# Loading an output projection over all 128 partitions in natural order, with one permuting product added

## The chip, the cores and the metric

The kernel runs on one core of one Trainium2 chip. The metric is the device time of one execution in microseconds (us). Every run is compared with runs of the kernel before on the same chip.

## The reference

A decode step of a gated mix of two branches. Only branch A matters here:

```python
x: (2, 1, 1024)   k_cache, v_cache: (2, 32, 16384, 128)   wq: (1024, 4096)   wo: (4096, 1024)   # bf16
q = (x @ wq) as (2, 32, 1, 128)
p = softmax(q . k_cache * 128 ** -0.5)
o = p . v_cache                                   # (2, 32, 1, 128)
a = o as (2, 1, 4096) @ wo
b = ...                                           # a small mixer and MLP branch
g = sigmoid((x * gate_w).sum(-1))
return g * a + (1 - g) * b
```

The two caches are 537 MB, so the kernel is a stream of cache tiles. `wo` (8.39 MB) comes last: nothing follows it but its own product and a 4 KB store.

One caution on correctness. Branch A averages 16,384 values and is, by the scales of the inputs, far smaller than branch B, so bf16 rounding of the output can hide it. That the changed kernel's permutation is right was therefore also worked through by index on random numbers in double precision (largest difference 1e-12).

## The kernel before

32 tiles of K and 32 of V, each [128 partitions, 32768] bf16, go through three buffers that `wo` shares. Everything is issued on one queue. Cuts are marked.

```python
WO_SPLIT = [16, 8, 4, 2, 1, 1]

def load_wo():
    t = big_tile("wo")[:].rearrange("p (r n) -> p r n", n=D)
    src = A_wo.rearrange("(h a r) n -> h a r n", a=4, r=32)      # head h, quarter a, row r in it
    r0 = 0
    for n in WO_SPLIT:
        for a in range(4):                                        # partition 32a + h
            nc.sync.dma_start(
                out=t[32 * a : 32 * a + 32, r0 : r0 + n, :], in_=src[:, a, r0 : r0 + n, :]
            )
        r0 += n
# ... (cut: other loads, K and V stages) ...
def wo_stage():
    Q = const.tile([P, B, 32], BF16)
    for b in range(B):
        nc.vector.transpose(out=Q[:, b, :], in_=OT[:, b, :])      # 32x32 blocks: Q[32a+h, b, r]
    wo = wt.pop("wo").rearrange("k r (p c) -> k r p c", c=KC)
    for r in range(32):
        for c in range(KC):                                       # 256 products
            nc.tensor.matmul(wo_acc[:, c, :], lhsT=wo[:, r, :, c], rhs=Q[:, :, r],
                             start=(r == 0 and c == 0), stop=(r == 31 and c == KC - 1))
# ... (cut) then fin = wo_acc * g, out_pm = fin + pre, one store
```

The transpose of 32x32 blocks leaves head h, quarter a on partition 32a + h. To meet it, `wo` is loaded in that order: four DMAs for each of six pieces, each to 32 neighbouring partitions.

## Time and profile before

Three runs gave a median of 1365.45 us (1365.17 to 1367.84).

| | kernel before |
|---|---|
| span of the profiled run | 1364.4 us |
| wo issued (the last K tile has been used, a buffer is free) | 1296.9 us |
| last V tile landed, its products begin | 1326.7 us |
| first half of wo landed | 1345.15 us |
| 256 wo products | 1345.4 to 1361.5 us |
| finish and store | 2.9 us |

The page's picture of the span, in 40 slices of 34 us. DMA is the busy share of 16 DMA engines in tenths, GB/s is what they moved:

```profile
DMA  9999999999999999999999999999999999999995
GB/s 400 439 442 431 429 431 423 437 431 439 429 437 431 431 435 437 431 429 429 429 433 444 431 431 433 429 431 435 437 429 429 433 431 437 441 431 430 431 255 139
```

The engines are busy until the last slice, so the memory queue bounds the kernel, but the last two slices move far less than 430 GB/s. The table of stretches shows that tail closer. Its columns are the stretch, its length, busy us of each engine (PE, PEld, which is PE's weight load, DVE, ACT, POOL) with the number of instructions, the granted TensorE clock, the DMA busy share, GB/s:

```profile
1280.00:1297.00 17.00, 15.14 (x54) 5.51 (x54) 15.85 (x14) 0.00 (x0) 0.00 (x0) 0.92 1.00 432
...
1310.00:1315.00 5.00, 0.00 (x0) 0.00 (x0) 0.00 (x0) 0.00 (x0) 0.00 (x0) 0.50 0.96 210
1315.00:1320.00 5.00, 0.00 (x0) 0.00 (x0) 0.00 (x0) 0.00 (x0) 0.00 (x0) 0.50 0.86 172
...
1330.00:1335.00 5.00, 3.34 (x44) 2.02 (x36) 0.37 (x2) 0.59 (x1) 0.00 (x0) 0.94 0.95 202
```

Read the last two columns together: a share of 0.96 with 210 GB/s says that packets are in flight but each takes twice as long. The packet records say it too: a 65,536-byte packet of a V tile takes 2.42 us in the stream and about 4.9 us (median) after 1305 us, once wo has begun. From 1335 to 1355 us the share is lower too, 0.61 to 0.68 at 133 to 204 GB/s: there some engines also stood idle.

The chain of waits that ended last (start us, us, what):

```profile
1296.92 0.34 SPq L127
...
1298.23 46.92 DMA wo<-in_A_wo_dram
1345.15 0.25 issue
1345.40 7.64 PE wo_acc L382 x125
1353.04 0.38 issue
1353.42 8.08 PE wo_acc L382 x131
1361.74 0.23 DVE out_pm L523
```

47 us of transfer and 16 us of products. In the timeline, the last V tile's products:

```profile
1326.73 5.56 PE L342 MATMUL O<-Vn,PT 128*32 128x512 bf16 x64 [19.22 <-DMA Vn<-in_A_v_cache_dram]
```

PE idled 19 us for that tile; the one before it had landed at 1295.2, and tiles come 19.4 us apart in the stream. So this tile too is late, by 12 us.

### The profile page before, as it was taken

What the parts mean: (1) busy time and instruction counts of PE and PEld (TensorE: products, weight loads), DVE (VectorE), ACT (ScalarE), POOL (GpSimd) and SP (SyncE); (2) the same over time, 40 slices, a digit from 0 to 9 for tenths busy, and PEclk for the clock granted to TensorE, in tenths of its full rate; (3) what the DMA queues carried; (4) which work ended last, traced back from release to release, by engine and by line L of the source; (5) the groups of instructions that cost most, each with busy time, mean ns of one, the idle gap of its engine ahead of it and who ended that gap; (6) DMA issues with size and microseconds to landing.
All of it is one profiled execution on the core that took longest, in us unless ns stands there. A gap on an engine that the chain in (4) does not pass through costs nothing.

```text
span 1364.4 us, 12947 instructions
## 1 busy us (share of the span) xinstructions
PE 829.0 (61%) x5523; PEld 401.0 (29%) x5586; DVE 707.2 (52%) x862; ACT 45.6 (3%) x100; POOL 14.5 (1%) x45
## 2 busy tenths in 40 slices
PE   2577665557665666555556755566656555666535
PEld 2233222423224232222223522232222222322215
DVE  0666656256661565654545445566555455666510
ACT  0000000000000000000000000000000000000000
POOL 0000000000000000000000000000000000000000
PEclk9988887688885888777778677888777788887766
DMA  9999999999999999999999999999999999999995
GB/s 400 439 442 431 429 431 423 437 431 439 429 437 431 431 435 437 431 429 429 429 433 444 431 431 433 429 431 435 437 429 429 433 431 437 441 431 430 431 255 139
DMA packets 11833, 573.36 MB, mean 420 GB/s; under 512 B 2176, under 2 KB 2176, under 8 KB 2560
## 3 DMA queue, kind: packets, MB, share of 16 engines
q1 hardware_dynamic: 11776, 572.54, 98.8%
q8 instruction: 43, 0.70, 0.2%
q14 instruction: 14, 0.11, 0.0%
HBM read 572.53 MB, written 0.00 MB: 420 GB/s over the span
## 4 chain that ended last, share of the span: by engine, by line
PE 28%; DVE 23%; DMA 20%; another core or an unknown queue 13%; issue 13%; ACT 2%; SPq 0%; ACTq 0%; POOL 0%
DVE T L290 19%; DMA Kn<-in_A_k_cache_dram 16%; PE S L298 14%; PE O L342 7%; DMA wo<-in_A_wo_dram 3%; PE misc L434 3%; PE misc L352 2%; PE misc L205 2%; ACT Pr L326 1%; DVE PT L330 1%; PE wo_acc L382 1%; ACT Os L350 1%; DVE mx L319 1%; DVE mdiag L312 1%
## 5 line engine op out<-in xcount | busy, mean ns | idle before, releaser
L298 PE MATMUL S<-T,z 128*128 128x512 bf16 x1985 | 583.6, 422 | 340.2 <-DVE T L290 320.4
L290 DVE STREAM_TRANSPOSE T<-Kn 128x1024 f32<-128x1024 f32 x512 | 611.8, 1229 | 267.5 <-DMA Kn<-in_A_k_cache_dram 217.2
L298 PEld LDWEIGHTS <-z 128*128 128x128 bf16 x2048 | 219.2, 107 | 699.2 <-issue 538.0
L342 PE MATMUL O<-Vn,PT 128*32 128x512 bf16 x2048 | 119.7, 387 | 19.2 <-DMA Vn<-in_A_v_cache_dram 19.2
L369 DVE TENSOR_TENSOR OT<-misc,rinv 128x2 bf16<-128x2 f32 x32 | 5.1, 159 | 171.0 <-PE misc L352 171.0
L342 PEld LDWEIGHTS <-PT 128*32 128x32 bf16 x2048 | 73.1, 140 | 65.2 <-DMA Vn<-in_A_v_cache_dram 19.3
L205 PE MATMUL misc<-rs,ones_f 128*128 128x2 f32 x64 | 17.9, 349 | 76.5 <-DVE rs L362 76.5
L350 ACT COPY Os<-O 128x512 f32<-128x512 f32 x32 | 18.8, 586 | 1100.9 <-PE O L342 1100.9
L352 PE MATMUL misc<-osel,Os 128*128 128x2 f32 x256 | 33.7, 254 | 22.2 <-ACT Os L350 22.2
L352 PEld LDWEIGHTS misc<-osel,Os 128*128 128x128 f32 x256 | 31.0, 191 | 36.7 <-ACT Os L350 36.7
L309 DVE TENSOR_REDUCE m<-S 128x1 f32<-128x512 f32 x32 | 22.2, 693 | 36.9 <-PE S L298 36.9
L434 PEld LDWEIGHTS <-wt 128*128 128x128 bf16 x576 | 35.7, 171 | 18.7 <-DMA wt<-in_B_w_dram 17.4
L205 PEld LDWEIGHTS misc<-rs,ones_f 128*128 128x128 f32 x64 | 16.1, 312 | 81.2 <-issue 78.4
L330 DVE STREAM_TRANSPOSE PT<-Pr 128x512 bf16<-128x512 bf16 x32 | 22.7, 711 | 28.7 <-ACT Pr L326 28.7
L326 ACT ACTIVATE Pr<-S,nb 128x512 bf16<-128x512 f32 x32 | 22.0, 687 | 124.4 <-DVE nb L321 121.4
L205 PE MATMUL misc<-mdiag,ones_f 128*128 128x128 f32 x64 | 15.6, 325 | 15.6 <-DVE mdiag L312 15.6
L319 DVE TENSOR_REDUCE mx<-misc 64x1 f32<-64x64 f32 x64 | 14.2, 222 | 19.0 <-PE misc L205 18.6
L268 POOL TENSOR_TENSOR z<-qsel,own 128x32 bf16<-128x32 bf16 x32 | 10.8, 338 | 1225.6 <-PE S L298 1194.3
L382 PE MATMUL wo_acc<-Q,wo 128*128 128x2 bf16 x256 | 15.7, 198 | 11.7 <-DMA wo<-in_A_wo_dram 11.4
L243 PE MATMUL misc<-xT,wt 128*128 128x2 bf16 x256 | 7.1, 165 | 25.8 <-DVE xT L238 23.1
L434 PE MATMUL misc<-xn2T,wt 128*128 128x2 bf16 x224 | 14.4, 202 | 9.1 <-DMA wt<-in_B_w_dram 9.1
L382 PEld LDWEIGHTS <-wo 128*128 128x128 bf16 x256 | 15.6, 169 | 11.8 <-issue 11.8
(70 smaller groups left out, 92.8 us busy)
## 6 DMA issues: line engine op xcount, KB each, us to landing
wt<-in_B_w_dram SPq DMA_DIRECT2D x2, 7168.0 KB, 50.4
wt<-in_B_w_dram SPq DMA_DIRECT2D x2, 2048.0 KB, 40.1
wo<-in_A_wo_dram SPq DMA_DIRECT2D x4, 1024.0 KB, 40.9
wo<-in_A_wo_dram SPq DMA_DIRECT2D x4, 512.0 KB, 49.1
wo<-in_A_wo_dram SPq DMA_DIRECT2D x4, 256.0 KB, 15.8
Kn<-in_A_k_cache_dram SPq DMA_DIRECT2D x32, 52.1
Vn<-in_A_v_cache_dram SPq DMA_DIRECT2D x32, 37.6
wo<-in_A_wo_dram SPq DMA_DIRECT2D x4, 128.0 KB, 6.0
```

Of the source, the lines that this page charges most:

```text
L205: nc.tensor.matmul(ps[:], lhsT=ones_f[:], rhs=src, start=True, stop=True)
L290: nc.vector.transpose(out=T[:].rearrange("p w j s -> p j w s"), in_=Kw[:, m * CW : (m + 1) * CW].rearrange("p (j w e) -> p j w e", w=2, e=32),
L298: nc.tensor.matmul(S[:], lhsT=z[:, v, NM - 1 - m : NM - 1 - m + P], rhs=Tb[:, v // 2, :, v % 2], start=(m == 0 and v == 0), stop=(m == NM ...
L309: nc.vector.reduce_max(out=m[:], in_=S[:], axis=AX.X)
L319: nc.vector.reduce_max(out=mx[pa, :], in_=mall[pa, pa], axis=AX.X)
L326: nc.scalar.activation(out=Pr[:], in_=S[:], func=ACTF.Exp, bias=nb[:], scale=scale, accum_out=rs[:])
L330: nc.vector.transpose(out=PT[:], in_=Pr[:])
L342: nc.tensor.matmul(O[32 * g : 32 * g + 32, :], lhsT=PT[:, m : CJ * 32 : 16], rhs=V[:, j0 : j0 + 4, :], start=(m == 0), stop=(m == NM - 1),)
L350: nc.scalar.copy(out=Os[:].rearrange("p x d -> p (x d)"), in_=O[:])
L352: nc.tensor.matmul(oc[:], lhsT=Os[:, x, :], rhs=osel[:, x, :], start=(x == 0), stop=(x == 3))
L382: nc.tensor.matmul(wo_acc[:, c, :], lhsT=wo[:, r, :, c], rhs=Q[:, :, r], start=(r == 0 and c == 0), stop=(r == 31 and c == KC - 1),)
L434: nc.tensor.matmul(ps[:, c, :], lhsT=w[:, r, :].rearrange("k (p c) -> k p c", c=C)[:, :, c], rhs=actT[:, r, :], start=(r == 0), stop=(r == ...
```

## The change

The intent: every DMA of wo writes all 128 partitions, as those of the K and V tiles do, which ran at 432 GB/s. In natural order partition p holds rows 32p to 32p + 31 of wo, that is head p // 4, quarter p % 4. The transposed head outputs have head h, quarter a on partition 32a + h; one product with a permutation matrix brings them to 4h + a.

```diff
 def load_wo():
-        src = A_wo.rearrange("(h a r) n -> h a r n", a=4, r=32)
+        src = A_wo.rearrange("(p r) n -> p r n", p=P)
         for n in WO_SPLIT:
-            for a in range(4):
-                nc.sync.dma_start(
-                    out=t[32 * a : 32 * a + 32, r0 : r0 + n, :], in_=src[:, a, r0 : r0 + n, :]
-                )
+            nc.sync.dma_start(out=t[:, r0 : r0 + n, :], in_=src[:, r0 : r0 + n, :])
 ...
+    perm = const.tile([P, P], BF16)
+    nc.vector.tensor_copy(
+        out=perm[:].rearrange("k (h a) -> k h a", a=4),
+        in_=ident_f[:].rearrange("k (a h) -> k h a", a=4),
+    )
 ...
 def wo_stage():
-        Q = const.tile([P, B, 32], BF16)
+        Q1 = const.tile([P, B, 32], BF16)
         for b in range(B):
-            nc.vector.transpose(out=Q[:, b, :], in_=OT[:, b, :])
+            nc.vector.transpose(out=Q1[:, b, :], in_=OT[:, b, :])
+        q_ps = misc_psum([P, B, 32])
+        nc.tensor.matmul(q_ps[:], lhsT=perm[:], rhs=Q1[:], start=True, stop=True)
+        Q = const.tile([P, B, 32], BF16)
+        nc.vector.tensor_copy(out=Q[:], in_=q_ps[:])
```

More of the change, by code (lines that the diff above doesn't have):

```diff
@@ L373, in wo_stage @@
     def wo_stage():
+        Q1 = const.tile([P, B, 32], BF16)
+        for b in range(B):
+            nc.vector.transpose(out=Q1[:, b, :], in_=OT[:, b, :])
+        q_ps = misc_psum([P, B, 32])
+        nc.tensor.matmul(q_ps[:], lhsT=perm[:], rhs=Q1[:], start=True, stop=True)
         Q = const.tile([P, B, 32], BF16)
-        for b in range(B):
-            nc.vector.transpose(out=Q[:, b, :], in_=OT[:, b, :])
+        nc.vector.tensor_copy(out=Q[:], in_=q_ps[:])
         wo = wt.pop("wo").rearrange("k r (p c) -> k r p c", c=KC)
```

## The prediction

> **What bounds the kernel now.** The memory queue. The page's slices show the 16 DMA engines at 0.9 or more and about 430 GB/s in nearly every slice; PE is busy 61%, DVE 52%. A K or V tile of 8.39 MB takes 19.4 us (landings 1275.9, 1295.2). Only the last two slices fall off: 255 and 139 GB/s. There wo is loaded, by 24 DMAs of 32 partitions. In the table of stretches the rate is 432 GB/s until 1297 us, 160 to 210 from 1310 to 1335, 130 to 200 after. The engines are occupied but slow: a 65,536-byte packet takes 4.8 us in place of 2.42. [...] The last V tile shares the queues with the first wo pieces and lands at 1326.7, not at the 1314.6 of the 19.4 us beat. The first half of wo (16 of 32 rows) lands at 1345.2, the last piece at 1359.7.
>
> The chain of waits at the end: wo issued 1296.9, DMA until 1345.15, 256 wo products 1345.4 to 1361.5 (60 ns a pair of weight load and product, granted clock 0.50, 0.4 us of waiting inside), then 2.9 us of finish and store.
>
> **What the change does.** 24 wo DMAs become 6 of 128 partitions, same bytes, same runs per row, still issued when the last K tile is consumed (about 1297). At the other tiles' beat V lands at 1314.6, the first half of wo 9.7 us later, 1324.3; the rest by about 1334 (estimates from 19.4 us).
>
> Added: a cast copy of the 128x128 matrix in the preamble (DVE idle: free); one 128x128 by 128x64 product and one 128x64 copy after the last head output. The trace's diagonal product costs 0.58 us from DVE to DVE; with a 0.2 us copy I estimate 0.8 to 1.0 us. V landing to head output takes 7.5 us (1326.73 to 1334.2), so head output at 1322.1, transposed 1322.4, Q ready about 1323.3: just before the first half of wo lands, so the addition is hidden, by about 1 us.
>
> wo products start at 1324.5; at 60 ns a pair they end at 1340.3. Every later piece has landed before it is needed: the tail turns from DMA-bound to PE-bound. Finish 2.9 us: span about 1343.2 against 1364.4, 21 us saved. Everything up to 1297 us is untouched.
>
> **Predicted time** 1344.5 us, 1.5% faster, range 1339 to 1351. Faster by over 2%: 0.10; within 2%: 0.89; slower: 0.01. Over 2% needs 27.3 us, for which the wo products would have to get cheaper.
>
> **Signs.** Right: no slice before the last one or two under 400 GB/s; 65,536-byte packets stay at 2.42 us to the end; last V landing near 1314.6; the wait before the first wo product 1 to 3 us (from 11.4); cadence still 60 ns; no waits between pieces.
>
> **What would make it wrong.** (a) The wo products may inherit the higher granted clock from the V products, since the gap shrinks from 11.4 to about 3 us; if 60 ns is set by the clock and not by the strided weights (unstrided ones at line 243 go at 26.7 ns), up to 6 us more is saved: 1338 to 1339, limited by wo's last landing. (b) wo at 128 partitions may run below 430 GB/s in small pieces; only the first half matters. (c) Q later than the first half: up to 1 us. (d) The one DMA engine that runs 1.7 us late delays every landing.

From 19.4 us a tile of the trace, V lands at 1314.6 and the first half of wo 9.7 us later; products from 1324.5 to 1340.3 and 2.9 us of finish give a span of 1343.2, and the predicted time was 1344.5 us.

## The result, and the profile after

The changed kernel takes 1345.78 us (median of four runs, 1345.74 to 1345.98) against 1365.76 for the kernel before (median of four runs). Ratio 0.9851, 95% interval 0.9834 to 0.9868. A ratio here is the mean time of one kernel's runs over the mean of the other's in the same rounds, so it is not quite the ratio of the medians quoted. 20 us are 1.5%: within 2%, and clear of the noise.

The same slices of the page, after:

```profile
DMA  9999999999999999999999999999999999999995
GB/s 406 434 435 432 435 437 423 433 434 432 432 432 440 426 435 432 424 433 435 435 436 428 436 435 434 423 433 438 436 426 433 432 432 433 432 432 435 435 430 220
```

Now only the last slice is short; from 1335.3 us on the products run with nothing left to load. The same columns of the table of stretches:

```profile
1280.00:1297.00 17.00, 14.86 (x57) 5.39 (x56) 15.91 (x14) 0.00 (x0) 0.00 (x0) 1.00 1.00 432
...
1310.00:1315.00 5.00, 0.00 (x0) 0.00 (x0) 0.00 (x0) 0.00 (x0) 0.00 (x0) 0.50 0.84 356
1315.00:1320.00 5.00, 4.32 (x44) 1.79 (x48) 0.00 (x0) 0.00 (x0) 0.00 (x0) 0.50 0.98 419
...
1330.00:1335.00 5.00, 5.00 (x86) 5.00 (x86) 0.00 (x0) 0.00 (x0) 0.00 (x0) 0.50 0.29 112
1335.00:1340.00 5.00, 5.00 (x87) 5.00 (x85) 0.00 (x0) 0.00 (x0) 0.00 (x0) 0.50 0.00 0
```

The chain of waits:

```profile
1296.20 29.18 DMA wo<-in_A_wo_dram
1325.39 0.05 issue
1325.43 15.55 PE wo_acc L388 x256
1340.98 0.02 issue
1341.00 0.19 DVE fin L527
...
1341.21 0.23 DVE out_pm L529
```

The transfer went from 47 to 29 us; the products keep their length, and no wait is left between them. The timeline shows the last V tile's products, the transpose, the added product and copy, and the start of the wo products:

```profile
1315.68 6.23 PE L344 MATMUL O<-Vn,PT 128*32 128x512 bf16 x64 [8.89 <-DMA Vn<-in_A_v_cache_dram]
...
1323.89 0.21 DVE L380 STREAM_TRANSPOSE Q<-OT 128x32 bf16<-128x32 bf16 x1
1324.15 0.19 PE L382 MATMUL misc<-Q,perm 128*128 128x64 bf16 x1 [0.50 <-DVE Q L380]
1324.38 0.23 DVE L384 CAST Q<-misc 128x64 bf16<-128x64 f32 x1 [0.28 <-PE misc L382]
...
1325.43 15.53 PE L388 MATMUL wo_acc<-Q,wo 128*128 128x2 bf16 x256 [1.09 <-DMA wo<-in_A_wo_dram]
```

Q is ready at 1324.61, the first half of wo at 1325.39: the added work hides behind the load with 0.8 us to spare.

Where the 20.4 us between the two spans come from, term by term:

| from the two chains | before | after | saved |
|---|---|---|---|
| wo issued | 1296.92 | 1296.20 | 0.7 (the part before, which the change leaves alone) |
| issue to landing of the first half | 48.23 | 29.19 | 19.0 |
| landing to first product | 0.25 | 0.04 | 0.2 |
| first to last product, with the wait inside | 16.10 | 15.55 | 0.55 |
| rest to the end of the span | 2.9 | 3.0 | -0.1 |

### The profile page after: what moved, and what is told of

Its sections match the earlier page's. It is cut to its first block, busy times and chain, and to the rows that moved or that the text cites. A ratio compares the mean times of both kernels' runs of the same rounds, so it can differ in the third digit from the quotient of the medians.

```text
span 1344.0 us, 12921 instructions
## 1 busy us (share of the span) xinstructions
PE 828.4 (62%) x5524; PEld 400.5 (30%) x5587; DVE 707.8 (53%) x864; ACT 45.6 (3%) x100; POOL 14.4 (1%) x45
## 4 chain that ended last, share of the span: by engine, by line
PE 28%; DVE 23%; DMA 19%; another core or an unknown queue 13%; issue 13%; ACT 2%; SPq 0%; ACTq 0%; POOL 0%
DVE T L292 20%; DMA Kn<-in_A_k_cache_dram 17%; PE S L300 13%; PE O L344 7%; PE misc L440 3%; DMA wo<-in_A_wo_dram 2%; PE misc L354 2%; PE misc L207 2%; ACT Pr L328 1%; DVE PT L332 1%; PE wo_acc L388 1%; ACT Os L352 1%; DVE mx L321 1%; DVE mdiag L314 1%
## 5 line engine op out<-in xcount | busy, mean ns | idle before, releaser
L440 PE MATMUL misc<-h2T,wt 128*128 128x2 bf16 x224 | 13.6, 198 | 7.9 <-DMA wt<-in_B_w_dram 7.9
L368 DVE RECIPROCAL rinv<-misc 128x2 f32<-128x2 f32 x32 | 5.5, 171 | 22.2 <-PE misc L207 22.2
```

The costliest lines, as they stand in the source:

```text
L440: nc.tensor.matmul(ps[:, c, :], lhsT=w[:, r, :].rearrange("k (p c) -> k p c", c=C)[:, :, c], rhs=actT[:, r, :], start=(r == 0), stop=(r == ...
```

## The experiments

Theory, the prediction's: a DMA that writes 32 neighbouring partitions is slow because of which partitions it writes, so the load of wo runs at about half the rate (210 and 202 GB/s in the stretches above, in place of 432), and slows the last V tile, which is in the queues at the same time. The first half of wo, landing late, held the chain. The product is hidden, and the tail is now bound by PE. Rivals: the permuted rows are slow to read from HBM; 24 DMAs are too many (they share eight semaphores; in the kernel before their queue waited 12 times for an earlier piece of wo, 24.6 us in all); 32 partitions are too few, whichever they are; and, for PE, that the clock and not the strided weights sets the 60 ns.

### Natural order, but 32 neighbouring partitions

```diff
-            nc.sync.dma_start(out=t[:, r0 : r0 + n, :], in_=src[:, r0 : r0 + n, :])
+            for a in range(4):
+                pa = slice(32 * a, 32 * a + 32)
+                nc.sync.dma_start(out=t[pa, r0 : r0 + n, :], in_=src[pa, r0 : r0 + n, :])
```

> The changed kernel with its natural order and its product kept, but each of the six pieces of wo again loaded by four DMAs of 32 neighbouring partitions (24 DMAs). Right result. Theory [...]: the loss comes back whole, about 1364 to 1367 us, rate 150 to 220 GB/s after 1310 us, 65,536-byte packets of the last V tile at 4.7 to 5 us. Rival (the permuted order reads HBM badly, rows 256 KB apart where the natural order has 64 KB): stays at 1345 to 1347 us, as the reading is now in natural order.

Measured: 1363.59 us (before in the same rounds 1365.71), ratio 0.9992, interval 0.9977 to 1.0006. The loss came back, the product notwithstanding. Two stretches of its table:

```profile
1310.00:1315.00 5.00, 0.00 (x0) 0.00 (x0) 0.00 (x0) 0.00 (x0) 0.00 (x0) 0.50 0.98 211
1330.00:1335.00 5.00, 4.04 (x44) 2.14 (x37) 0.20 (x2) 0.59 (x1) 0.00 (x0) 0.80 0.96 203
```

These are 211 and 203 GB/s where the kernel before had 210 and 202, now read in natural order: the reading order is not the cause. Its median is under the expected 1364 by 0.4 us; the first half landed at 1343.45 in place of 1345.15, which lies in the spread that the kernel before shows (1363.9 to 1366.7 in these rounds).

### 32 partitions, every fourth

```diff
-            nc.sync.dma_start(out=t[:, r0 : r0 + n, :], in_=src[:, r0 : r0 + n, :])
+            for a in range(4):
+                nc.sync.dma_start(out=t[a : P : 4, r0 : r0 + n, :], in_=src[a : P : 4, r0 : r0 + n, :])
```

> The changed kernel, each piece of wo loaded by four DMAs of 32 partitions, each taking every fourth partition (a, a+4, ..., a+124) in place of 32 neighbours: same number of DMAs, same bytes each, same rows read by each as in the kernel before. Right result. Theory [...] 1344 to 1349 us and no slow packets. Rivals (32 partitions a DMA are too few; 24 DMAs are too many; rows read 256 KB apart are slow): about 1365 us, as before.

Measured: 1357.88 us, ratio 0.9948 (0.9933 to 0.9962): neither number. The timeline tells why:

```profile
1315.70 5.51 PE L347 MATMUL O<-Vn,PT 128*32 128x512 bf16 x64 [8.31 <-DMA Vn<-in_A_v_cache_dram]
...
1337.74 15.50 PE L391 MATMUL wo_acc<-Q,wo 128*128 128x2 bf16 x256 [14.09 <-DMA wo<-in_A_wo_dram]
```

The V tile landed as early as in the changed kernel, the first half of wo too (1325.38 against 1325.39), and all of wo had landed at 1337.5 (1335.3 in the changed kernel); packets of 65,536 and 32,768 bytes stayed at 2.42 and 1.21 us (4.9 and 2.5 us with 32 neighbours in the kernel before). The rate is full: from 1312 to 1320 us 414 GB/s, against 422 in the changed kernel and 214 in the kernel before. The rows that each DMA reads are those of the kernel before; only the partitions written differ. But the first product starts at 1337.74, after the last piece. The author's reading is that the program's tracking of which product reads which write can't tell these striped pieces apart; the built program that would show it is not among the records. So the theory is confirmed by the rate and the expected time was missed for a reason of the experiment's own. The reversed order, further down, checks that reading.

### 24 DMAs of 128 partitions

```diff
+        flat = big_tile("wo")[:]                          # t is a view of it
+        src_flat = A_wo.rearrange("(p r) n -> p (r n)", p=P)
 ...
-            nc.sync.dma_start(out=t[:, r0 : r0 + n, :], in_=src[:, r0 : r0 + n, :])
+            w = n * D // 4
+            for q in range(4):
+                c0 = r0 * D + q * w
+                nc.sync.dma_start(out=flat[:, c0 : c0 + w], in_=src_flat[:, c0 : c0 + w])
```

> The changed kernel with each piece of wo cut into four DMAs of 128 partitions and a quarter of the columns: 24 DMAs of the same bytes as in the kernel before. Right result. Theory: within 2 us of the changed kernel (1345 to 1349 us), the later pieces issued late but still landed in time. Rival (the number of DMAs, their issue one by one behind eight semaphores): most of the 20 us comes back, 1358 to 1366 us.

Measured: 1345.69 us, ratio 0.9855 (0.9839 to 0.9872), as the changed kernel. Neither the number of DMAs, nor their size, nor the queueing for semaphores (the last was issued at 1335.6) matters here: the first half of wo landed at 1325.7, the last piece at 1337.7, 2.4 us after that of the changed kernel, which the products hid.

### Two halves of 64 partitions

```diff
-            nc.sync.dma_start(out=t[:, r0 : r0 + n, :], in_=src[:, r0 : r0 + n, :])
+            for a in range(2):
+                pa = slice(64 * a, 64 * a + 64)
+                nc.sync.dma_start(out=t[pa, r0 : r0 + n, :], in_=src[pa, r0 : r0 + n, :])
```

> The changed kernel with each piece of wo loaded by two DMAs of 64 neighbouring partitions (12 DMAs). Right result. Theory [...]: as slow as 32 neighbours, 1360 to 1367 us. Rival (rate goes with the number of partitions): half of the loss or none, 1345 to 1356 us.

Measured: 1365.40 us, ratio 1.0003 (0.9988 to 1.0018); the same two stretches of its table:

```profile
1310.00:1315.00 5.00, 0.00 (x0) 0.00 (x0) 0.00 (x0) 0.00 (x0) 0.00 (x0) 0.50 0.91 198
1330.00:1335.00 5.00, 3.64 (x53) 2.35 (x45) 0.50 (x3) 0.59 (x1) 0.00 (x0) 0.99 0.95 202
```

Twice the partitions, the same rate. With every fourth of 128 fast and 64 neighbours slow, what counts is which partitions, not how many.

### Without the added product

```diff
-        q_ps = misc_psum([P, B, 32])
-        nc.tensor.matmul(q_ps[:], lhsT=perm[:], rhs=Q1[:], start=True, stop=True)
-        Q = const.tile([P, B, 32], BF16)
-        nc.vector.tensor_copy(out=Q[:], in_=q_ps[:])
+        Q = Q1
```

> The changed kernel without its added product: the wo products take the transposed head outputs as they are. WRONG RESULT on purpose (wo's rows meet the wrong heads). In the changed kernel's trace Q is ready at 1324.6 us and the first half of wo lands at 1325.4. Theory (the product is hidden): the same within 0.5 us, 1345.3 to 1346.2. Rival (the product lies on the chain): 0.8 to 1.0 us faster.

Measured: 1345.96 us (1345.63 to 1347.16), against 1345.78 with it, in other rounds. The product costs nothing that can be measured.

### Neighbouring columns as weights, in both kernels

```diff
-        wo = wt.pop("wo").rearrange("k r (p c) -> k r p c", c=KC)
+        wo = wt.pop("wo").rearrange("k r (c p) -> k r p c", c=KC)
```

> The changed kernel with the weights of each wo product taken as 128 neighbouring columns of wo in place of every eighth. WRONG RESULT on purpose (output columns permuted). Theory (stride sets the 60 ns; the changed kernel's tail is bound by PE): cadence about 27 ns, the tail becomes bound by the last landing of wo at 1335.3, so 4.5 to 5.5 us faster, 1340 to 1341.5 us. Rival (the granted clock of 0.5 or something per instruction sets the 60 ns): cadence 60 ns and 1345.7 us.

Measured in the changed kernel: 1340.93 us, ratio to the kernel before 0.9824 (0.9810 to 0.9837), 4.9 us less than the changed kernel, and 5.0 us less than the run without the product, which shares its chip. Its timeline:

```profile
1325.41 3.57 PE L388 MATMUL wo_acc<-Q,wo 128*128 128x2 bf16 x128 [2.16 <-DMA wo<-in_A_wo_dram]
1330.25 1.87 PE L388 MATMUL wo_acc<-Q,wo 128*128 128x2 bf16 x64 [1.28 <-DMA wo<-in_A_wo_dram]
...
1335.32 0.37 PE L388 MATMUL wo_acc<-Q,wo 128*128 128x2 bf16 x8 [0.28 <-DMA wo<-in_A_wo_dram]
```

128 products in 3.57 us are 28 ns each (27 between starts), and each piece is now waited for: DMA binds again, and its last piece lands at 1335.3.

> The same edit in the kernel before. WRONG RESULT on purpose. Theory (there the tail is bound by DMA): the last piece lands at 1359.65 and products ended at 1361.5, so only 1 to 2 us faster, 1363.5 to 1364.8 us; the products then wait between pieces. Rival (PE bounds the tail in both kernels): as many us as in the changed kernel, 1358 to 1361 us.

Measured in the kernel before: 1365.15 us, ratio 1.0001 (0.9987 to 1.0014), no gain that can be told from the noise where 1 to 2 us were expected (the interval leaves room for at most 1.8 us). The products did get as fast (125 recorded in 3.47 us) and waited between pieces:

```profile
1345.26 3.47 PE L382 MATMUL wo_acc<-Q,wo 128*128 128x2 bf16 x125 [11.70 <-DMA wo<-in_A_wo_dram]
...
1360.74 0.35 PE L382 MATMUL wo_acc<-Q,wo 128*128 128x2 bf16 x8 [1.79 <-DMA wo<-in_A_wo_dram]
```

The last small piece landed at 1360.33 here and at 1359.65 in the profile of before, which used up most of the gain. That PE did not bind the tail of the kernel before is confirmed; the expected gain was not seen.

### A right version of it

The diff, cut to its core: w4 (and a second set of w2 products) also take neighbouring columns; x is loaded a second time as 16 rows of 128 and transposed by PE; the output is turned back.

```diff
+        nc.sync.dma_start(out=x_rows[:], in_=A_x.rearrange("b s (c p) -> (b s c) p", p=P))
 ...
-        wo = wt.pop("wo").rearrange("k r (p c) -> k r p c", c=KC)
+        wo = wt.pop("wo").rearrange("k r (c p) -> k r p c", c=KC)
 ...
+        nc.vector.tensor_tensor(out=pre[:], in0=xC[:], in1=linear("w2", shT, blocks=True)[:], op=ALU.add)
 ...
-        nc.vector.tensor_tensor(out=pre[:], in0=x1[:], in1=linear("w4", h2T)[:], op=ALU.add)
+        nc.vector.tensor_tensor(out=pre[:], in0=pre[:], in1=linear("w4", h2T, blocks=True)[:], op=ALU.add)
 ...
-        nc.sync.dma_start(out=out.rearrange("b s (p r) -> p (b s) r", p=P), in_=out_pm[:])
+    nc.tensor.matmul(rows_ps[:], lhsT=out_pm[:].rearrange("p b r -> p (b r)"), rhs=perm[:], start=True, stop=True)
+    nc.vector.tensor_copy(out=out_rows[:].rearrange("m (a h) -> m h a", a=4),
+                          in_=rows_ps[:].rearrange("m (h a) -> m h a", a=4))
+    nc.sync.dma_start(out=out.rearrange("b s (c p) -> (b s c) p", p=P), in_=out_rows[:])
```

> A right version of that: the changed kernel with wo's weights taken as 128 neighbouring columns, the other branch's result brought to the same order (x read a second time as 16 rows and transposed by PE, w2 and w4 products also with neighbouring columns), and the output turned back to rows by one product with the permutation matrix before its store. Right result. Theory: tail bound by the last landing at about 1335.3, plus about 0.7 us for the added product and copy: 1340.5 to 1342 us, 3.5 to 5 us faster than the changed kernel and 1.75 to 1.9% faster than before. Rival (the added steps at the end or at the start cost what is won): 1344 to 1346 us.

Measured: 1341.08 us (five runs, 1341.01 to 1341.14), ratio 0.9825 (0.9812 to 0.9839). It beats both kernels: 24.0 us under the median of before in its rounds, 4.7 us under the changed kernel, and 4.9 us under the run without the product, which shares its chip. (Its ratio's interval touches that of the changed kernel, because the kernel before scatters; the times of these kernels themselves lie apart.) The last wo products end at 1335.5; the turning back costs 1.1 us, of which the copy in permuted order is 0.70.

### The wo products in reverse order

```diff
-        for r in range(32):
+        for r in reversed(range(32)):
 ...
-                    start=(r == 0 and c == 0),
-                    stop=(r == 31 and c == KC - 1),
+                    start=(r == 31 and c == 0),
+                    stop=(r == 0 and c == KC - 1),
```

> The changed kernel with the wo products taken in reverse order of rows, so that the first product waits for the last and smallest piece. Right result. It is the control for the run that loaded every fourth partition, where the first product waited for all pieces (its tracking of writes could not tell them apart). Theory (that run lost its time to this wait alone, not to its rate): first product at about 1335.3, end of span 15.5 + 3 us later, 1354 us; time 1355.5 to 1356.5 us, and the run with every fourth partition is slower than this by no more than its later last landing (2.2 us). Rival (loading every fourth partition is itself slow): this one is much under 1355 us.

Measured: 1355.68 us (two runs), span 1353.8. First product at 1335.14, right after the last landing. The run with every fourth partition has a span of 1356.2, 2.4 us more, and its last piece landed 2.4 us later (1337.50 against 1335.09). The 24 DMAs of 128 partitions ended as late (1337.70). So its whole distance from the changed kernel is that wait plus the later end that comes with 24 DMAs; nothing is left for a slower rate.

### The wo products at a higher clock

```diff
+        spin(wt["wo"][:, 0, 0:512], 24)         # 24 idle products of 512 columns into a spare bank
         wo = wt.pop("wo").rearrange("k r (p c) -> k r p c", c=KC)
         for r in range(32):
+            if r % 4 == 3:
+                spin(wo[:, 0, 0:64, :], 1)
```

> The changed kernel with 24 idle products of 512 columns put just before the wo products (they wait for the first half of wo) and one more before every fourth row, so that the wo products run at a granted clock of 1.0. Right result. Theory (the stride of the weights sets 60 ns): cadence between the idle products stays 58 to 62 ns at clock 1.0; added time about 24 idle products (7 us) and 8 more (1.7 us), 1353 to 1356 us. Rival (the clock sets it): cadence 27 to 45 ns and 1346 to 1350 us. Inconclusive if the records show a clock of 0.5 throughout.

Measured: 1355.57 us (two runs). The table of stretches for the line of the wo products alone (us, PE busy and count, weight loads busy and count, clock, DMA share, GB/s):

```profile
1330.00:1335.00 5.00, 2.05 (x33) 2.21 (x34) 0.97 0.27 105
1335.00:1340.00 5.00, 4.68 (x76) 4.69 (x76) 0.72 0.01 3
1340.00:1345.00 5.00, 4.52 (x74) 4.53 (x74) 0.50 0.00 0
```

At a clock of 0.97 a product takes 2.05 / 33 = 62 ns, at 0.50 it takes 4.52 / 74 = 61 ns (both with the edges of their groups; the median between starts is 60.0 in both). The chain of waits shows the idle products (S) as a check on the clock:

```profile
1334.44 0.24 PE S L379
1334.68 1.88 PE wo_acc L397 x32
...
1340.99 0.45 PE S L379
1341.44 1.86 PE wo_acc L397 x32
```

An idle product takes 0.24 us first and 0.45 us later, when the clock has halved, but 32 wo products take 1.88 and 1.86 us. The clock makes no difference to them. Together with the neighbouring columns, which took 27 ns at clock 0.50, this settles that the step of eight elements between weights sets the 60 ns.

### The kernel before, its four blocks issued in another order

```diff
-            for a in range(4):
+            for a in (0, 2, 1, 3):
```

> The kernel before with only the issue order of the four 32-partition blocks changed: 0, 2, 1, 3 in place of 0, 1, 2, 3, so that neighbouring DMAs in the queue write to different halves of the partitions (0 to 63 and 64 to 127). Right result, no product. Theory ([...] engines that have run ahead work on the next DMA, in the other half): part of the loss comes back, as the engines are up to 8 us apart: 1350 to 1362 us. If all engines worked on the same DMA at all times: no change, 1364 to 1367 us. Rival (32 partitions are slow by themselves): no change.

Measured: 1363.08 us against 1365.06, ratio 0.9985 (0.9969 to 1.0002): at most a small gain, not clear of the noise, and under the expected 3 us. In its profile the first half of wo landed at 1341.99, 3.2 us earlier than in the profile of before, while the rate from 1310 to 1335 stayed at 164 to 226 GB/s. (wo was also issued 0.9 us earlier in it, at 1296.05.) Different halves in neighbouring DMAs of one queue did not add up to the full rate; that they would was the assumption, and no trace before this run showed it. Nor is it that the engines never overlap. The kept trace has 16 updates of a semaphore for each of these DMAs (no view above prints them), read here as the ends of the 16 engines' shares. Seven of them came by 1311.0 us for the first block of this run (partitions 0 to 31), and from 1323.5 to 1325.5 for its fourth (96 to 127). The other nine came for the first block only from 1324.5 to 1330.0. So from about 1320 to 1324 us both halves were being written, and the rate from 1320 to 1325 was 187 GB/s. Why they do not add up stays open.

## Why the prediction was right

- **The bound and the cause.** The load of wo at half rate (160 to 210 GB/s) was named as the cause. Shown: 32 or 64 neighbouring partitions bring the whole loss back, in natural order too; every fourth partition gives the full rate with the same count, sizes and rows; 24 DMAs of 128 partitions are as fast as 6. Which partitions a DMA writes decides the rate in these runs. Why neighbouring ones are slow is not shown; two halves written at once in the last run did not add up to the full rate.
- **The landings.** V tile predicted at 1314.6, measured 1315.6; first half of wo predicted at 1324.3, measured 1325.4. Both are 1 us late, because the estimate took the usual 19.4 us from V tile to V tile where the last took 20.3; this is most of the 1.3 us by which the time was over the prediction (about 0.5 us of it is time outside the profiled span, and the shorter products took back 0.25). Why that interval was 1 us longer was not tested.
- **The product hidden by about 1 us.** 0.8 us in the trace, and nothing measurable when it is taken out.
- **The tail bound by PE, 60 ns a pair.** 15.55 us for 256 in place of the estimated 15.8, no wait between pieces. Making the products faster gained 4.9 us after the change and nothing measurable before it.
- **The named risk, that 60 ns depends on the clock.** In the kernel before, the granted clock was 0.94 from 1330 to 1335 us, with V products, and 0.50 under the wo products. The gap before the wo products did shrink, to 1.1 us, but the clock did not carry over: it was 0.84 from 1320 to 1325 us and 0.50 in all of them, while they kept PE busy for 15.5 us. It would not have helped: at clock 0.97 the cadence is the same (60.0 ns).
- **The last V tile's 12 us.** Correctly seen as lost and won back (11 us of the 12), and correctly not added as a gain of its own; it enters only as the moment from which wo's 9.7 us are counted. The head outputs were ready at 1334 in the kernel before, 11 us before the first half of wo. Only the landing of wo was on the chain.

## What to carry to other kernels

Look for DMA engines that are busy while GB/s drops: that pair of columns tells slow packets from a lack of work, and here the cure was in the shape of the transfer. Shape a load for the partitions (from 1312 to 1320 us here 214 GB/s with 32 neighbours a DMA, 414 with every fourth, 422 with all 128) and put the reordering on the small operand, where one product of 64 columns and its copy took 0.5 us from transpose to ready, and hid. When a load at the end of the kernel has been mended, look at once at the compute behind it: here weights taken at a step of eight elements cost 60 ns a product in place of 27, which was worth nothing measurable before the change and 4.9 us after it.
